# One head pair's loads in 14 DMAs instead of 30, key and value tiles laid out alike for both halves of a query tile, and a new order of issue

## The chip, the core and the metric

The kernel runs on one core of a Trainium2 chip. The metric is the device time of one execution in microseconds (us), the median of several runs; a profiled execution of the same program gives the trace. Engines are named as the profile names them: PE is the matrix engine (PEld its weight loads), DVE the vector engine, ACT the scalar engine, POOL GpSimd, SP the engine that here issues every DMA.

## The reference, cut to what matters

The inputs hold 4 batches of 8 heads. Each head has 512 local and 32 global queries, keys and values of 64 numbers, all float32.

```python
s_g   = scale * q_g @ [k_g, k_l].T                    # 32 global queries see all 544 keys
out_g = softmax(s_g) @ [v_g, v_l]
s_ll  = where(|i - j| <= 32, scale * q_l @ k_l.T, -1e9)  # 512 local queries: a band of 65 local keys ...
s_l   = [scale * q_l @ k_g.T, s_ll]                    # ... and the 32 global keys
out_l = softmax(s_l) @ [v_g, v_l]
x     = [out_g, out_l]                                 # 4 x 544 tokens of 512
h = x @ w_in;  x = (h * tanh(softplus(h))) @ w_out     # first feed-forward, 512 -> 2048 -> 512
h = x @ w2_in; out = (h * cos(h)) @ w2_out             # second feed-forward
```

The feed-forward weights arrive as 64-bit floats and are converted on the chip.

## The kernel before, in words

The work falls into two parts. **Attention** runs over 16 pairs of heads (`pp`, two heads of one batch; `NP` is 16). **Feed-forward** follows, in groups of two of the 16 blocks of the hidden width, each a product in three passes on rounded halves of the numbers (`l1` at L581 to L583, `l2` at L702). The first matmuls of the feed-forward (7 calls of `ff`) and the first 8 of 64 weight conversions (`c0` to `d5`, with loads at L137) are mixed into the attention part.

What a pair does, by the step names of the table `ORDER`: `lq` loads queries and keys (L292), `lv` loads values (L307). `Q` and `K` transpose them on PE, `q`, `k` and `h` copy the results out of PSUM. Queries lie in 4 tiles of 128 (`m`), each with two halves of 64 (`e`); a half sees 128 local keys and the 32 global ones, 160 columns. `S` (L370) makes the scores of two tiles of both heads in 8 matmuls, `X` masks and exponentiates, `ne`, `ni`, `N` and `NB` normalize (POOL and DVE), `TA` and `TB` transpose the probabilities of local and global keys, `ta` and `tb` copy them, and `AV` (L436) multiplies by the values: per half one matmul with local values (`ve` for even halves, `vo` for odd) and one with the global ones. For the global queries `SG`, `sm`, `st`, `se`, `ss`, `si`, `sn`, `TG` and `tg` do the same for two pairs at once (`m`), and `AG` multiplies by the values. `lg`, `G` and `g` load and transpose the global queries and keys of a batch, and `kg` copies the global keys into the key tile.

In the key tile `kw` the 160 columns of an even half are its 128 local keys and then the 32 global ones; an odd half's columns begin 64 further on, so that its global keys lie in the midst of its local ones. Its rows of probabilities have that order too, and therefore the value tiles have it: `vo` holds global values in its middle rows, and the 32 local values that come last lie in a fourth tile, `vx`. The keys are loaded shifted by 32, with wrap-around, in three pieces for each head.

What sets the order: each engine runs its instructions in the order in which the steps stand in `ORDER`, a table written into the code and read at L554. The letter behind a step's number puts its copy on ACT (`a`) or DVE (`d`). SP issues all DMAs in that order too, so a load that waits for its buffer holds up all loads behind it. Buffers: two for queries and keys (`qn`, `kn`, `kw`, `QT`), three for values. A value load therefore waits for `AV` and `AG` three pairs back.

Of the kernel before, what the change touches and what calls it, by code (L numbers as in the profile page):

```python
# [9 lines left out]
F32 = mybir.dt.float32  # L10
# [53 lines left out]
def kernel(  # L64
# [38 lines left out]
    def setup(mask):  # L103

        nc.gpsimd.memset(magic[:, 0:1], MAGIC)
        nc.gpsimd.memset(magic[:, 1:2], -MAGIC)
        nc.gpsimd.memset(mask, 0.0)
        band = [(0, 0, 128, 1, 0), (0, 0, 128, -1, 64), (64, 0, 64, 1, 0), (64, 96, 160, -1, 0)]
        for row, c0, c1, sgn, base in band:
            part = mask[row:row + 64, 1, c0:c1]  # L110
            nc.gpsimd.affine_select(
# [152 lines left out]
    def attention(ap, ps, pss, conv, tail):  # L264
# [12 lines left out]
        for t in kw:  # L277
            nc.vector.memset(t[:, NJ * W + 32:NJ * W + 64], 0.0)
# [552 lines left out]
```

## Time and profile before

| | |
|---|---|
| median of 3 runs | 1030.34 us (1029.53 to 1031.15) |
| profiled execution, its own time | 1031.32 us |
| its span, first to last instruction | 1028.4 us |
| PE busy | 918.7 us (89%) |
| DVE busy | 660.7 us (64%) |
| ACT busy | 455.9 us (44%) |
| POOL busy | 86.9 us (8%), all of it in the attention part |

The time of the profiled execution is 2.9 us longer than its span. Shares over the whole span say little here, since the attention part and the feed-forward part have different limits: the page's strip of slices shows PE at 3 to 7 tenths in the first quarter and at 9 after it. So each part is read by itself. "Waited for" in a row names the instruction that came last; idle time of an engine counts only where no other engine was the limit.

### The profile page before, as it was taken

Reading aid. Unit: us, or ns where it says so; the run is one execution under the profiler, and the core shown is the slowest. Engines: PE = TensorE matmul, PEld = TensorE weight load, DVE = VectorE, ACT = ScalarE, POOL = GpSimd, SP = SyncE. Lnnn points to the kernel's source line nnn. Section 1 sums busy time; section 2 is a strip of 40 time slices with the busy share of each in tenths; the row PEclk is TensorE's granted clock in tenths of the full one; section 3 lists DMA queues with packets and bytes.
Section 4 is the critical chain, followed back from the end, with each engine's and each line's share of the span. In section 5 each row is a group of like instructions: output and inputs, shape, how many; then the busy total and the mean of one; then the engine's idle time right before and its main releaser. Section 6 shows DMA issues by size and latency. Waiting matters only on the chain.

```text
span 1028.4 us, 16927 instructions
## 1 busy us (share of the span) xinstructions
PE 918.7 (89%) x6491; PEld 848.7 (83%) x6491; DVE 660.7 (64%) x1321; ACT 455.9 (44%) x907; POOL 86.9 (8%) x138
## 2 busy tenths in 40 slices
PE   4376665657889999999999999999999999999998
PEld 3254553546889999999999999999999999999997
DVE  2365634535599886878987784555655556666565
ACT  2154432524555444445443342554555554544443
POOL 3053422414000000000000000000000000000000
PEclk6668867868999999999999999999999999999999
DMA  3463343343233544597644457300000260000001
GB/s 81 97 146 85 71 96 78 70 97 71 74 103 98 169 164 162 191 345 290 199 148 158 147 164 265 124 1 1 1 1 1 98 230 1 32 31 32 1 31 51
DMA packets 117855, 108.06 MB, mean 105 GB/s; under 512 B 82832, under 2 KB 99216, under 8 KB 117776
## 3 DMA queue, kind: packets, MB, share of 16 engines
q1 hardware_dynamic: 117776, 107.00, 33.4%
q8 instruction: 51, 0.84, 0.3%
q14 instruction: 28, 0.23, 0.1%
HBM read 77.33 MB, written 29.62 MB: 104 GB/s over the span
## 4 chain that ended last, share of the span: by engine, by line
PE 78%; SPq 11%; DMA 4%; DVE 3%; issue 2%; ACT 1%; POOL 0%; POOLq 0%; ACTq 0%
PE acc L702 36%; PE h L581 12%; PE h L583 12%; PE h L582 12%; DMA qn<-in_q_l_dram 2%; SPq L323 2%; SPq L322 2%; SPq L318 1%; DMA cs<-in_moe_w_in_dram 1%; PE av L445 1%; PE av L449 1%; PE s L378 1%; SPq L317 1%; PE avg L517 1%; SPq L319 1%
## 5 line engine op out<-in xcount | busy, mean ns | idle before, releaser
L581 PE MATMUL h<-xl,w 128*128 128x384 f32 (+1 forms) x768 | 251.7, 328 | 2.9 <-DVE xl L571 2.9
L583 PE MATMUL h<-xh,w 128*128 128x384 f32 (+1 forms) x768 | 251.5, 327 | 0.0
L582 PE MATMUL h<-xh,w 128*128 128x384 f32 (+1 forms) x768 | 251.4, 327 | 0.0
L702 PE MATMUL acc<-gh,w 128*128 128x384 f32 (+1 forms) x768 | 186.0, 326 | 1.0 <-DVE w L219 1.0
L702 PE MATMUL acc<-w,gh 128*128 128x512 f32 x544 | 169.0, 392 | 0.0
L581 PEld LDWEIGHTS h<-xl,w 128*128 128x128 f32 x768 | 145.5, 189 | 5.1 <-DVE xl L571 3.2
L582 PEld LDWEIGHTS h<-xh,w 128*128 128x128 f32 x768 | 145.4, 189 | 1.8
L583 PEld LDWEIGHTS h<-xh,w 128*128 128x128 f32 x768 | 145.5, 189 | 0.0
L702 PEld LDWEIGHTS acc<-gh,w 128*128 128x128 f32 x768 | 135.5, 188 | 1.3 <-DVE w L219 1.3
L702 PE MATMUL acc<-gl,w 128*128 128x384 f32 (+1 forms) x384 | 125.1, 326 | 0.4 <-DVE xT L521 0.4
L702 PEld LDWEIGHTS acc<-w,gh 128*128 128x128 f32 x544 | 102.1, 188 | 20.5
L702 PE MATMUL acc<-w,gl 128*128 128x512 f32 x272 | 105.9, 389 | 0.0
L609 ACT ACTIVATE w<-h 128x768 f32<-128x768 f32 (+1 forms) x48 | 37.4, 778 | 142.3 <-PE h L583 137.1
L638 DVE SCALAR_TENSOR_TENSOR w<-w,h 128x768 f32<-128x768 f32 (+2 forms) x49 | 43.8, 894 | 71.4 <-ACT w L634 71.4
L628 DVE SCALAR_TENSOR_TENSOR w<-k,h 128x768 f32<-128x768 f32 (+2 forms) x49 | 43.8, 894 | 66.2 <-ACT k L627 66.2
L626 ACT ACTIVATE k<-h,magic 128x768 f32<-128x768 f32 (+2 forms) x49 | 41.9, 856 | 98.2 <-PE h L583 97.7
L345 PE MATMUL qt<-ident,qn 128*128 128x128 f32 x64 | 15.9, 399 | 74.8 <-DMA qn<-in_q_l_dram 74.8
L633 ACT ACTIVATE w<-w 128x768 f32<-128x768 f32 (+2 forms) x49 | 39.1, 798 | 89.1 <-DVE w L629 89.1
L345 PEld LDWEIGHTS qt<-ident,qn 128*128 128x128 f32 x64 | 11.0, 205 | 78.0 <-issue 61.8
L397 ACT ACTIVATE pr<-pr,nm 128x160 f32<-128x160 f32 x128 | 53.2, 418 | 48.4 <-DVE nm L394 46.3
L702 PEld LDWEIGHTS acc<-gl,w 128*128 128x128 f32 x384 | 72.4, 188 | 0.5 <-ACT xT L545 0.5
L614 DVE TENSOR_TENSOR gl<-w,gh 128x768 fp32r<-128x768 f32 (+1 forms) x48 | 43.6, 909 | 33.1 <-ACT gh L610 33.1
(115 smaller groups left out, 1405.7 us busy)
## 6 DMA issues: line engine op xcount, KB each, us to landing
scr<-co SPq DMA_DIRECT2D x48, 512.0 KB, 3.0
w<-scr SPq DMA_DIRECT2D x48, 512.0 KB, 5.3
cs<-in_moe_w_in_dram SPq DMA_DIRECT2D x32, 512.0 KB, 4.4
cs<-in_moe_w_out_dram SPq DMA_DIRECT2D x32, 512.0 KB, 4.2
out_dram<-o SPq DMA_DIRECT2D x17, 256.0 KB, 2.0
qn<-in_q_l_dram SPq DMA_DIRECT2D x32, 128.0 KB, 2.6
kn<-in_k_l_dram SPq DMA_DIRECT2D x32, 96.0 KB, 2.3
ve<-in_v_l_dram SPq DMA_DIRECT2D x32, 96.0 KB, 2.2
```

The costliest lines, as they stand in the source:

```text
L345: nc.tensor.transpose(t[:, j, :], qk[pp][0][:, j], ident)
L397: nc.scalar.activation(out=pr[:, i], in_=pr[:, i], func=AF.Exp, bias=nm[:, i:i + 1], scale=-1.0, accum_out=l[:, i:i + 1])
L581: nc.tensor.matmul(ps[:, c, 0:n], wh[:, k, :], xl[k], start=(k == 0), stop=False)
L582: nc.tensor.matmul(ps[:, c, 0:n], wh[:, k, :], xh[k], start=False, stop=False)
L583: nc.tensor.matmul(ps[:, c, 0:n], wl[:, k, :], xh[k], start=False, stop=(k == NK - 1))
L609: nc.scalar.activation(out=w, in_=h, func=AF.Mish)
L614: nc.vector.tensor_tensor(out=gl, in0=v["w"], in1=gh.bitcast(F32), op=ALU.subtract)
L626: nc.scalar.activation(out=k, in_=h, func=AF.Identity, scale=INV2PI, bias=magic[:, 0:1])
L628: nc.vector.scalar_tensor_tensor(out=t, in0=k, scalar=-C1, in1=h, op0=ALU.mult, op1=ALU.add)
L633: nc.scalar.activation(out=t, in_=t, func=AF.Sin, scale=0.5)
L638: nc.vector.scalar_tensor_tensor(out=t, in0=t, scalar=1.0, in1=h, op0=ALU.subtract, op1=ALU.mult, reverse0=True)
L702: nc.tensor.matmul(o, l, r, start=(g == 0 and m == 0), stop=(g == G - 1 and m == 5))
```

## The change

A pair is loaded in 14 DMAs. Keys come unshifted, one DMA for each head. Values of both heads are loaded together, in 6 DMAs for `ve` and `vo` and 4 for `vg`; the tile `vx` goes. The key tile becomes 8 blocks of 160 columns, one for each half, each with its local keys first and the global ones last; three copies fill the local part (`k`: blocks 1 to 3, the new step `k2`: blocks 4 to 6, `h`: 96 columns of blocks 0 and 7), and `kg` copies the global keys into 8 blocks instead of 4. With both halves ordered alike, `AV` does the global keys of a whole tile in one matmul of 128 columns for each head, ahead of the local ones. `SG` needs one more small matmul for each pair, since 32 local keys now come from the last block. `sn` moves from POOL to ACT or DVE, by its letter. The mask follows the new order. `ORDER` is a new table, 665 steps instead of 649; the number of conversions and of `ff` calls in it is the same.

```diff
 ORDER = """
-    hot:-1 hot:19 lq:0 setup lg:0 lv:0 Q:0 q:0a G:0 lq:1 g:0 K:0 k:0a kg:0 h:0a kg:1 S:0 lv:1 X:0 S:1 lq:2 Q:1 X:1 K:1
+    hot:-1 hot:19 lq:0 Q:0 K:0 q:0d lg:0 k:0a setup G:0 k2:0a g:0 c0:0 kg:0 lq:1 h:0a S:0 Q:1 c2:0 K:1 c1:0 kg:1 X:0
...
-        vx = [ap.tile([P, NJ - 1, 2, D], F32, name=f"vx{i}") for i in range(3)]
-        kw = [ap.tile([P, NJ * W + 64], F32, name=f"kw{i}") for i in range(2)]
+        kw = [ap.tile([P, 2 * NJ, W], F32, name=f"kw{i}") for i in range(2)]
...
             for h in range(2):
-                k = k_l[b, h0 + h]
-                nc.sync.dma_start(out=kn[32:P, 0, h], in_=k[0:P - 32])
-                nc.sync.dma_start(out=kn[:, 1:NJ, h, :], in_=k[P - 32:SL - 32].rearrange("(c p) d -> p c d", p=P))
-                nc.sync.dma_start(out=kn[0:32, 0, h], in_=k[SL - 32:SL])
+                nc.sync.dma_start(out=kn[:, :, h, :], in_=k_l[b, h0 + h].rearrange("(c p) d -> p c d", p=P))
...
         def load_v(pp):
...
+            v = v_l[b, 2 * p:2 * p + 2].rearrange("h s d -> (h s) d")
+            g = v_g[b, 2 * p:2 * p + 2]
+            both = v.rearrange("(c p) d -> p c d", p=P)
+            nc.sync.dma_start(out=E[32:P].rearrange("p h m d -> p (h m) d"), in_=both[0:P - 32])
             for h in range(2):
-                v, g = v_l[b, 2 * p + h], v_g[b, 2 * p + h]
-                rows = v.rearrange("(m p) d -> p m d", p=P)
-                nc.sync.dma_start(out=E[:, 1:NJ, h], in_=v[P - 32:SL - 32].rearrange("(m p) d -> p m d", p=P))
-                nc.sync.dma_start(out=E[32:P, 0, h], in_=v[0:P - 32])
-                nc.sync.dma_start(out=E[0:32, 0, h], in_=v[SL - 32:SL])
-                nc.sync.dma_start(out=O[0:64, :, h], in_=rows[32:96])
-                nc.sync.dma_start(out=O[96:P, :, h], in_=rows[96:P])
-                nc.sync.dma_start(out=O[64:96, :, h], in_=g[:, None, :].to_broadcast([SG, NJ, D]))
-                for jl in range(2):
-                    i = 2 * jl + h
-                    nc.sync.dma_start(out=G[32 * i:32 * i + 32, i], in_=g)
-                    nc.sync.dma_start(out=X[32 * i:32 * i + 32, jl:NJ - 1:2, h], in_=rows[0:32, jl + 1:NJ:2])
+                nc.sync.dma_start(out=E[0:32, h, 1:NJ], in_=both[P - 32:P, NJ * h:NJ * h + NJ - 1])
+            nc.sync.dma_start(out=E[0:SG, :, 0], in_=g.rearrange("h p d -> p h d"))
+            nc.sync.dma_start(out=O[0:P - 32].rearrange("p h m d -> p (h m) d"), in_=both[32:P])
+            nc.sync.dma_start(out=O[P - 32:P].rearrange("p h m d -> p (h m) d")[:, 0:2 * NJ - 1], in_=both[0:32, 1:2 * NJ])
+            for i in range(4):
+                nc.sync.dma_start(out=G[SG * i:SG * i + SG, i], in_=g[i % 2])
...
-        def k_copy(pp):
-            w, t = kw[pp % 2], live["k", pp]
-            copy("k", pp, w[:, 0:NJ * W].rearrange("p (m c) -> p m c", c=W)[:, :, 0:P], t)
-
-        def k_halo(pp):
-            w, t = kw[pp % 2], live["k", pp]
-            copy("h", pp, w[:, NJ * W:NJ * W + 32], t[:, 0, 0:32])
+        def k_copy(pp, j=1):
+            t = live["k", pp].rearrange("p a c -> p (a c)")
+            src = bass.AP(tensor=t.tensor, offset=t[:, 64 * j - 32:].offset, ap=[t.ap[0], [64, 3], [1, P]])
+            copy("k", pp, kw[pp % 2][:, j:j + 3, 0:P], src)
+
+        def k_copy2(pp):
+            k_copy(pp, 4)
...
         def av_pe(pp):
...
             for m in range(NJ):
                 jj, jl = divmod(m, 2)
+                for h in range(2):
+                    nc.tensor.matmul(av[pp][64 * h:64 * h + 64, m, :], G[:, 2 * jl + h, :], PB[pp][:, jj, :], start=True, stop=False)
                 for e in range(2):
                     cols = slice(64 * e, 64 * e + 64)
-                    last = e == 0 or m < NJ - 1
                     for h in range(2):
-                        nc.tensor.matmul(av[pp][64 * h:64 * h + 64, m, cols], (O if e else E)[:, m, h, :],
-                                         PA[2 * pp + jj][:, 2 * jl + h, cols], start=True, stop=not last)
-                    if last:
-                        for h in range(2):
-                            nc.tensor.matmul(av[pp][64 * h:64 * h + 64, m, cols], X[:, m, h, :] if e else G[:, 2 * jl + h, :],
-                                             PB[pp][:, jj, cols], start=False, stop=True)
+                        nc.tensor.matmul(av[pp][64 * h:64 * h + 64, m, cols], (O if e else E)[:, h, m, :],
+                                         PA[2 * pp + jj][:, 2 * jl + h, cols], start=False, stop=e == 1)
...
         def sg_norm(m):
-            nc.gpsimd.tensor_scalar(out=sgt, in0=sgt, scalar1=live["gr", m], scalar2=None, op0=ALU.mult)
+            if engine["at"] == "a":
+                nc.scalar.activation(out=sgt, in_=sgt, func=AF.Copy, scale=live["gr", m])
+            else:
+                nc.vector.tensor_scalar(out=sgt, in0=sgt, scalar1=live["gr", m], scalar2=None, op0=ALU.mult)
```

How this stands on the engines, at three places. First SP, in the first third of the attention part. Before, behind the query DMAs of one pair: the three key DMAs of its second head, then the first head's values (`ve`, `vo`, `vg`, `vx`), of which two more rows and the second head's ten follow.

```order
L302 DMA kn<-in_k_l_dram 96x64
L303 DMA kn<-in_k_l_dram 128x3x64
L304 DMA kn<-in_k_l_dram 32x64
L314 DMA ve_88<-in_v_l_dram 128x3x64
L315 DMA ve_88<-in_v_l_dram 96x64
L316 DMA ve_88<-in_v_l_dram 32x64
L317 DMA vo_91<-in_v_l_dram 64x4x64
L318 DMA vo_91<-in_v_l_dram 32x4x64
L319 DMA vo_91<-in_v_g_dram 32x4x64
L322 DMA vg_94<-in_v_g_dram 32x64
L323 DMA vx_97<-in_v_l_dram 32x2x64
```

Now SP at about the same place, queries and keys of a pair and then all values of a pair:

```order
L301 DMA qn<-in_q_l_dram 128x4x64 x2
L303 DMA kn<-in_k_l_dram 128x4x64 x2
L315 DMA ve_88<-in_v_l_dram 96x8x64
L317 DMA ve_88<-in_v_l_dram 32x3x64 x2
L318 DMA ve_88<-in_v_g_dram 32x2x64
L319 DMA vo_91<-in_v_l_dram 96x8x64
L320 DMA vo_91<-in_v_l_dram 32x7x64
L322 DMA vg_94<-in_v_g_dram 32x64 x4
```

Fourteen issues stand where 30 stood; the largest, of 96x8x64, are twice the size of any value DMA before. Over the whole program SP's list has 293 rows in place of 596.

Second PE, at the `AV` step of the third pair. Before, behind the `AG` step of another pair, the matmuls of one query tile (`ve` and `vo` local values, `vg` and `vx` global ones and the rest; `PA`, `PB` the transposed probabilities):

```order
L517 MATMUL avg<-PG,ve_89 64x32 x8
L517 MATMUL avg<-PG,vo_92 64x32 x2
L445 MATMUL av<-PA,ve_90 64x64 x2
L449 MATMUL av<-PB,vg_96 64x64 x2
L445 MATMUL av<-PA,vo_93 64x64 x2
L449 MATMUL av<-PB,vx_99 64x64 x2
```

Now, the same work of one query tile of another pair, behind a transpose and a score step:

```order
L425 MATMUL ta<-ident,pr 128x128 x4
L382 MATMUL s<-kw_98,QT 64x160 x8
L446 MATMUL av<-PB,vg_94 64x128 x2
L450 MATMUL av<-PA,ve_88 64x64 x2
L450 MATMUL av<-PA,vo_91 64x64 x2
```

Two matmuls of 128 columns stand in place of four of 64; the last tile of a pair had no `vx` rows before, so a pair goes from 30 matmuls to 24.

Third ACT. Before, a key copy and its 32 columns (`kw<-kt`), a query copy and the exponentials of the global queries (`sg`), then those of the local ones (`pr`); the multiplication of `sg` by `gr` (L494) stood on POOL:

```order
L545 COPY kw_100<-kt 128x4x128
L545 COPY kw_100<-kt 128x32
L545 COPY QT<-qt 128x512
L482 ACTIVATE sg,gl<-sg_1124,gnm 128x512
L483 ACTIVATE sg,gl<-sg_1125,gnm 128x32
L397 ACTIVATE pr,l<-pr,nm 128x160 x8
```

Now, a stretch of ACT's list with the same kinds of work:

```order
L142 ACTIVATE ca<-cs 128x512
L550 COPY QT<-qt 128x512
L550 COPY kw_98<-kt 128x3x128
L497 ACTIVATE sg<-sg,gr 128x640
L401 ACTIVATE pr,l<-pr,nm 128x160 x4
L550 COPY PB<-tb 128x256
```

A key copy of 384 columns (one of two, with a third of 192) and the multiplication of `sg` stand on ACT; over the part, six of the eight multiplications are on ACT and two on DVE.

## Rows read from the trace of the kernel before

**Rows 1.** The view by windows: attention up to the first second-layer matmul of the feed-forward, the 28.6 us behind it, and the rest. Columns: window, length, busy time of each engine (instructions), granted PE clock, share of the DMA engines, GB/s.

```profile
0.00:271.40 271.40, 169.72 (x2273) 134.32 (x2274) 127.33 (x490) 104.52 (x367) 86.89 (x138) 0.77 0.38 89
271.40:300.00 28.60, 25.71 (x139) 25.39 (x138) 23.84 (x42) 14.66 (x29) 0.00 (x0) 0.94 0.24 74
300.00:1028.40 728.40, 723.28 (x4083) 688.98 (x4081) 509.52 (x790) 336.72 (x513) 0.00 (x0) 1.00 0.33 112
```

**Rows 2.** The view of waits in the attention part: engine and line, what it waited for, us in total, times, longest.

```profile
PE qt L345 <- DMA qn<-in_q_l_dram: 74.8, 11, 10.1
...
PE av L449 <- DMA vg<-in_v_g_dram: 5.3, 3, 2.5
...
PE av L445 <- DMA ve<-in_v_l_dram: 2.1, 1, 2.1
```

**Rows 3.** SP's timeline: start, length, issue. A conversion load, then one pair from its query DMAs on, and the next pair's; last the first conversion load behind all attention loads, with the wait for its buffer.

```profile
34.35 1.73 SPq L137 DMA_DIRECT2D cs<-in_moe_w_in_dram  x1
...
175.43 0.97 SPq L299 DMA_DIRECT2D qn<-in_q_l_dram  x2
176.50 0.45 SPq L302 DMA_DIRECT2D kn<-in_k_l_dram  x1
176.99 0.43 SPq L303 DMA_DIRECT2D kn<-in_k_l_dram  x1
177.46 0.48 SPq L304 DMA_DIRECT2D kn<-in_k_l_dram  x1
...
181.00 0.61 SPq L317 DMA_DIRECT2D vo<-in_v_l_dram  x1
181.65 0.60 SPq L318 DMA_DIRECT2D vo<-in_v_l_dram  x1
182.29 0.43 SPq L319 DMA_DIRECT2D vo<-in_v_g_dram  x1
...
190.10 0.97 SPq L299 DMA_DIRECT2D qn<-in_q_l_dram  x2
...
261.20 22.73 SPq L137 DMA_DIRECT2D cs<-in_moe_w_in_dram  x4
```

**Rows 4.** SP's own waits over the whole run: the longest in total of those that belong to loads of a pair (waited for, us in total, times, longest).

```profile
SPq L314 <- PE avg L517: 3.5, 1, 3.5
```

**Rows 5.** PE's timeline: the first `S` step of the run, the first and last instructions of one `AV` step, the two kinds of matmul of an `SG` step, and a `Q` and an `S` step behind a wait. Columns: start, length, form, count, and in brackets the idle time before with what ended it.

```profile
9.21 1.83 PE L378 MATMUL s<-kw,QT 64*64 64x160 f32 x18 [0.75 <-ACT kw L545]
...
84.24 0.34 PE L445 MATMUL av<-PA,ve 128*64 128x64 f32 x4
...
85.92 0.29 PE L445 MATMUL av<-PA,vo 128*64 128x64 f32 x4
...
88.94 0.31 PE L463 MATMUL sg<-kw,qz 128*64 128x32 f32 x4
89.08 1.06 PE L466 MATMUL sg<-kw,qz 128*64 128x512 f32 x4
...
100.55 1.09 PE L345 MATMUL qt<-ident,qn 128*128 128x128 f32 x4 [9.39 <-DMA qn<-in_q_l_dram]
101.57 1.35 PE L378 MATMUL s<-kw,QT 64*64 64x160 f32 x16
```

**Rows 6.** The view by windows again, columns as in Rows 1: two stretches in which loads were ahead, a third at full clock, and a starved one.

```profile
51.40:90.60 39.20, 32.99 (x464) 25.11 (x464) 30.10 (x118) 24.57 (x93) 20.43 (x29) 0.80 0.47 113
...
72.00:91.00 19.00, 18.61 (x303) 15.01 (x301) 16.10 (x67) 12.06 (x47) 10.53 (x16) 0.86 0.24 54
183.00:200.00 17.00, 14.35 (x228) 10.34 (x227) 11.73 (x53) 10.33 (x41) 8.61 (x14) 0.99 0.32 72
...
140.00:160.00 20.00, 10.50 (x138) 7.99 (x138) 7.72 (x35) 5.71 (x25) 5.47 (x10) 0.73 0.39 93
```

**Rows 7.** Groups of instructions of the attention part, by line and form: busy us and mean ns, then idle time before and what ended it. Two of PE, then copies on DVE and ACT, exponentials on ACT, and three of POOL.

```profile
L360 PE MATMUL kt<-ident,kn 128*128 128x128 f32 x64 | 11.6, 310 | 3.7 <-DMA kn<-in_k_l_dram 1.3 <-issue 1.2 <-DVE nm L394 0.6
...
L333 PE MATMUL gt<-ident,gq 64*128 64x64 f32 x16 | 2.0, 254 | 1.3 <-DMA gq<-in_k_g_dram 1.2
...
L547 DVE COPY kw<-kt 128x512 f32<-128x512 f32 x7 | 4.8, 684 | 2.6 <-PE kt L360 2.6
...
L547 DVE COPY PB<-tb 128x256 f32<-128x256 f32 x8 | 3.3, 415 | 1.2 <-PE tb L430 1.1
...
L547 DVE COPY kw<-kt 128x32 f32<-128x32 f32 x11 | 2.0, 181 | 0.5 <-ACT kw L545 0.5
...
L397 ACT ACTIVATE pr<-pr,nm 128x160 f32<-128x160 f32 x128 | 53.2, 418 | 48.4 <-DVE nm L394 46.3 <-POOL pb L415 1.8 <-POOL pr L410 0.2
...
L545 ACT COPY kw<-kt 128x512 f32<-128x512 f32 x9 | 5.3, 584 | 7.7 <-PE kt L360 7.6
...
L410 POOL TENSOR_TENSOR pr<-pr,r 128x512 f32<-128x512 f32 x32 | 35.3, 1103 | 31.8 <-DVE r L406 28.1 <-DVE kw L547 1.8 <-PE ta L421 1.3
L494 POOL TENSOR_SCALAR sg<-sg,gr 128x640 f32<-128x640 f32 x8 | 16.2, 2028 | 12.8 <-DVE gr L491 12.7
...
L355 POOL COPY kw<-kG 128x128 f32<-128x128 f32 x15 | 4.7, 328 | 24.6 <-PE sg L463 15.9 <-PE s L378 3.4 <-DVE kG L340 3.2
```

**Rows 8.** DMA issues of the page: KB each, and median us from issue to landing.

```profile
qn<-in_q_l_dram SPq DMA_DIRECT2D x32, 128.0 KB, 2.6
...
ve<-in_v_l_dram SPq DMA_DIRECT2D x32, 96.0 KB, 2.2
```

More of the change, by code (lines that the diff above doesn't have):

```diff
@@ L107, in setup @@
         nc.gpsimd.memset(mask, 0.0)
[L108 to L111, printed above, removed]
-                out=part, in_=part, pattern=[[sgn, c1 - c0]], compare_op=ALU.is_ge, fill=NEG,
-                base=base, channel_multiplier=-sgn)
+        for row in (0, 64):
+            for sgn, base in ((1, 0), (-1, 64)):
+                part = mask[row:row + 64, 1, 0:P]
+                nc.gpsimd.affine_select(
+                    out=part, in_=part, pattern=[[sgn, P]], compare_op=ALU.is_ge, fill=NEG,
+                    base=base, channel_multiplier=-sgn)
         for m in (0, 2):
@@ L116, in setup @@
         nc.gpsimd.memset(mask[0:64, 0, 0:32], NEG)
[L117 removed]
+        nc.gpsimd.memset(mask[64:128, 2, 96:128], NEG)
     slots = {}
@@ L277, in attention @@
         for t in kw:
-            nc.vector.memset(t[:, NJ * W + 32:NJ * W + 64], 0.0)
+            nc.vector.memset(t[:, 0, 0:32], 0.0)
+            nc.vector.memset(t[:, 2 * NJ - 1, 96:128], 0.0)
         nc.vector.memset(sgt[:, SL:SL + P], 0.0)
-        for t in vg + vx:
+        for t in vg:
             nc.gpsimd.memset(t, 0.0)
+        for t in vo:
+            nc.gpsimd.memset(t[96:P, 1, NJ - 1], 0.0)
         NP = B * NPAIR
@@ L459, in sg_pe @@
             t0 = pss[0].tile([P, NJ, P], F32, tag="s", name="sg0", bufs=3)
-            t1 = ps_t([P, SG], "sg1")
+            t1 = ps_t([P, 2 * SG], "sg1")
             live["sg", m] = t0, t1
             for c in range(2):
-                nc.tensor.matmul(t1[64 * c:64 * c + 64], qz[b % 2][:, p + c, :], kw[c][:, P:W], start=True, stop=True)
+                for i, at in enumerate((P, 64)):
+                    nc.tensor.matmul(t1[64 * c:64 * c + 64, SG * i:SG * i + SG], qz[b % 2][:, p + c, :], kw[c][:, 2 * NJ - 1, at:at + SG], start=True, stop=True)
             for c in range(2):
-                keys = kw[c][:, 0:NJ * W].rearrange("p (m c) -> p m c", c=W)[:, :, 0:P]
-                nc.tensor.matmul(t0[64 * c:64 * c + 64], qz[b % 2][:, p + c, :], keys, start=True, stop=True)
+                nc.tensor.matmul(t0[64 * c:64 * c + 64], qz[b % 2][:, p + c, :], kw[c][:, 0:2 * NJ:2, 0:P], start=True, stop=True)
         def sg_max(m):
```

91 lines of the change are left out of this document (48 added, 43 removed).

## The prediction

> **What bounds the kernel now.** I read the run by parts, then the waits of the busiest engine, then the queue that it waits for.
>
> The windows part the run [rows 1]. From 271.4 us on, PE is busy 25.71 + 723.28 = 749 of 757 us: PE is the limit there, and the change touches nothing in it. In the first 271.4 us PE is busy 169.72 us at a mean granted clock of 0.77, DVE 127.33, ACT 104.52, POOL 86.89, and the DMA engines 38%. No engine is near full, so something between them is the limit.
>
> PE is idle 271.4 - 169.7 = 101.7 us there. The waits say for what [rows 2]: 74.8 us at `Q` for the query DMA, in 11 waits of up to 10.1 us, and 5.3 + 2.1 us at `AV` for values. Two groups add 1.3 us for keys and 1.2 us for global ones [rows 7]. Loads together cost PE 84.7 us; all else leaves 17.0 us.
>
> Why do queries come late? In SP's timeline one issue follows another about 0.47 us apart, with hardly a gap [rows 3], and SP's own waits for a free buffer are 3.5 us at the line that waits longest [rows 4]. The pair that begins at 175.43 holds SP until 190.10. Thirty issues of 0.42 to 0.61 us make 14.1 us, and 16 pairs 226 of the 261.2 us after which SP is through [rows 3]. A query DMA lands 2.6 us after its issue [rows 8], so the landing is short; what is late is the issue, behind twenty value DMAs. **SP's issuing bounds the attention part**, at 271.4 / 16 = 17 us for each pair.
>
> **The change, part by part.** *SP.* A pair has 14 issues. The four of queries and keys have shapes the trace shows, 0.49 us apart: 2.0 us. Of the ten for values the four `vg` are known, and 32-row pieces cost 0.43 to 0.60 us. A 96x8x64 issue isn't in the trace. Nearest are the three-dimensional value issues of 0.60 and 0.61 us, and above them the longest conversion issue without a wait, 1.73 us [rows 3]. I take 0.61, since 128x4x64 (0.49) isn't dearer than 32x4x64 (0.60): cost doesn't follow size. Ten value issues come to 4.8 us, a pair to 6.8 us, 16 pairs to 109 us. With 8 global loads (3.7 us), 8 conversion loads (some 6 us) and half of the odd stalls before (261 - 226 - 10 = 25 us, so 13 us), SP needs about 132 us instead of 261. The work that was behind it now counts.
>
> *PE.* Its work in the part is 169.72 us at 0.77, or 131 us at full clock. `AV` goes from 30 matmuls of 64 columns to 16 of 64 and 8 of 128. At full clock 15 groups of two take 85.92 - 84.24 = 1.68 us plus the last, 0.12 us each [rows 5]; a doubled column count makes 16 such units, so +0.12 us a pair, +2 us in all: no saving, since columns cost and not matmuls. From below, an instruction's fixed share could save: 6 of 30 matmuls, at most 0.35 us a pair. `SG` gets as many small matmuls again, 0.14 us a step [rows 5], +1 us. Sum 134 us at full clock (126 to 134).
>
> *DVE.* Before it made 7 key copies at 684 ns and 11 of 32 columns at 181, 6.8 us; now 15 of 384 columns and 10 of 192. Between the 256-column row (415) and the 512-column row [rows 7] I estimate 550 and 350 ns: 11.8 us, +5.0. At the rates of these rows, three `QT`, three `PB`, one `xT` copy and one conversion step that go to ACT or behind the part take off 2.1 + 1.2 + 0.7 + 0.8 = 4.8. Two `sn` come at some 0.8 us: +1.6. Net +2, so 129 us.
>
> *ACT.* 17 key copies at an estimated 480 ns and 6 at 280 make 9.8 us against 6.2: +3.6. Copies taken over +1.7, one conversion step less -0.6, six `sn` at about 0.7 us +4.2. Sum 104.5 + 9 = 113 us.
>
> *POOL.* The eight `sn` of 2.03 us go (-16.2 us); fifteen `kg` copies double from 328 ns (+4 to 5 us) [rows 7]. Sum 75 us. `sn` also leaves a chain: POOL waited 12.7 us for it.
>
> *The rest of the run.* Conversions and `ff` calls in the table are the same, so I price the 757 us at 0, covered by PE being busy in 749 of them; one or two us either way.
>
> **How long the part becomes.** PE and DVE are now the largest, and both have a record of what they reach when loads are ahead [rows 6]. By PE: in 72 to 91 us it was busy 98% at a clock of 0.86. 134 / 0.86 = 156 us, plus the 17 us of waits that weren't loads, is 173. By DVE: 30.10 of 39.2 us busy from 51.4 to 90.6, 77%, so 129 / 0.77 = 168. I take **170 us**, a gain of 101 us.
>
> The bounds: at a clock of 0.99, as from 183 to 200 [rows 6], PE needs 135 us, and with some 10 us of start, since the first scores begin at 9.21 [rows 5], the part can't end ahead of 145. At 0.73, as from 140 to 160, PE needs 184 us, with the 17 us 201.
>
> The profiled execution took 1031.3 us, 1.0 above the median, so I count from the median: 1030.3 - 101 = **929 us**; bounds 1030.3 - 126 = 904 and 1030.3 - 70 = 960.
>
> **The rivals.**
>
> *PE stays at its lower clock.* The new order leaves short gaps, and PE runs much of the part at 1.2 GHz, as in the starved stretch. For it: even in 51.4 to 90.6 the clock was 0.80. Against: where PE had no waits of 8 us for queries, the clock was 0.86 to 0.99 [rows 6]. At the part's own 0.77: 134 / 0.77 + 17 = 191, a gain of 80: 950 us, up to the 960 above.
>
> *The large issues are dear.* Two 96x8x64 issues a pair at 1.73 us instead of 0.61 add 16 x 2 x 1.12 = 36 us to SP's 132, 168 us, and then 10 us of tail as before (271.4 - 261.2): 178, but with the starved pattern left in parts, some 185: 944 us. Against it stands that no row's issue time grows with size.
>
> *The transfers were the limit, not the issues.* The bytes hardly change, so the part would stay 271 us: about 1030 us, no change. Against it: the DMA engines are busy 38% of the part [rows 1]; in 170 us the same bytes would make it some 60%. The Trainium skill, in "DMA: Bandwidth & Descriptors", section "Issuing engines are not separate DMA queues", speaks for this rival: the time on the sequencer to start a DMA "is usually small relative to the DMA itself". The trace doesn't bear that out here, since one issue after another at 0.47 us apart outlasts landings of 2.2 to 2.6 us that overlap.
>
> *SP blocks itself: slower than before.* A value load waits for `AV` and `AG` three pairs back, and the next pair's query DMA is queued behind it on SP, with PE, DVE and ACT waiting for that. If each pair became one chain: 6.8 us of issue, 2.6 of landing, `Q` 1.1 and `S` 1.35 [rows 5], four exponentials 1.7, one `pr` of POOL 1.1 [rows 7], three copies at 0.6, `TA` some 1, `AV` 1.8: 19 us. It decides from 17 us a pair on; at 19 us the part is 304 us and the time 1063 us. Against it: in the new table every value load stands at least 21 steps behind the steps it waits for, at 170 / 665 = 0.26 us a step some 5 us.
>
> That the change doesn't do what it says is excluded by SP's list: 293 rows against 596.
>
> **How the numbers follow.** Forecast (part of 145 to 185 us, 904 to 944) 0.74; lower clock 0.16; dear issues 0.06; transfers 0.02; self-blocking 0.02. The range of 904 to 960 takes in the first three as priced and leaves out the last two and what lies beyond the bounds, less than 2 in 10. A measurement of this kernel can tell about 0.2% (2 us) from no change. Faster 0.74 + 0.16 + 0.06 = 0.96, same 0.02, slower 0.02.
>
> **What would show it.** SP's timeline: 14 issues a pair, about 7 us, with waits for `AV` or `Q` now between them; the 96x8x64 issue at 0.4 to 0.7 us. PE's wait for query DMAs down from 74.8 to under 15 us. The first second-layer matmul at about 170 us instead of 270.4. In that part PE busy over 80% at a clock above 0.8, DVE busy about 129 us, POOL 75. From there to the end 757 us as before. The forecast is wrong if `Q` still waits for loads while SP issues without gaps, if the part ends after 200 us with PE's clock at 0.77 or lower, or if the feed-forward part changes its length by more than a few us.

## The result, and the profile after

| | before | changed |
|---|---|---|
| median, us (lowest to highest, runs) | 1030.74 (1029.53 to 1033.55, 4) | 923.34 (922.06 to 924.07, 4) |
| profiled execution, us (its span) | 1031.3 (1028.4) | 924.07 (922.3) |
| first matmul of the second layer, us | 270.4 | 164.9 |
| from there to the end of the span, us | 758.0 | 757.4 |

The ratio is 0.8953 (95% interval 0.8932 to 0.8975): 107 us less, or 10.5%. Nearly all of it lies in the attention part, which ends 105.5 us sooner; the rest keeps its length to 0.6 us.

Windows of the changed kernel, cut where the second layer begins. The columns are length, then busy time and count of PE, PEld, DVE, ACT and POOL, PE's mean granted clock, the DMA engines' share and GB/s; they answer to [rows 1].

```profile
0.00:164.94 164.94, 137.79 (x2108) 112.78 (x2109) 129.14 (x495) 111.34 (x385) 74.42 (x130) 0.94 0.65 141
193.50:922.30 728.80, 724.07 (x4087) 689.80 (x4085) 509.96 (x791) 336.78 (x513) 0.00 (x0) 1.00 0.33 112
```

PE now is busy 137.79 of 164.94 us, 84%, at a clock of 0.94 instead of 0.77. Its idle time fell from 101.7 us to 27.2. In units of full clock its work is 137.79 x 0.94 = 129.5 us, before 131. This product is rough: for kernels below with the same matmuls it comes to between 125 (e1) and 133 us (e11). So far as it can tell, the work is the same, and both the waits and the clock gave time back. Behind the part, in the second row, PE is busy 724.07 of 728.80 us as before. The DMA share rose from 0.38 to 0.65, with nearly the same bytes in less time.

PE's waits in that part (line, what it waited for, total us, times, longest), which answer to [rows 2]:

```profile
PE qt L344 <- DMA qn<-in_q_l_dram: 7.7, 3, 6.5
PE kt L358 <- DMA kn<-in_k_l_dram: 6.8, 4, 4.4
PE av L446 <- DMA vg<-in_v_g_dram: 5.8, 2, 4.3
PE s L382 <- DVE kw L353: 1.4, 1, 1.4
PE tg L504 <- ACT sg L497: 1.2, 1, 1.2
```

Waits for loads are 20.3 us instead of 84.7, and spread over queries, keys and global values. They are few and long (up to 6.5 us). All other waits come to some 7 us. So the loads are still what PE waits for most.

SP's timeline of one pair, from its queries on (start, duration, line, operation, what is loaded, how many issues), which answers to [rows 3], and the first issue behind the last pair:

```profile
83.61 1.83 SPq L322 DMA_DIRECT2D vg<-in_v_g_dram  x4
85.49 0.97 SPq L301 DMA_DIRECT2D qn<-in_q_l_dram  x2
86.51 1.86 SPq L303 DMA_DIRECT2D kn<-in_k_l_dram  x2
88.42 0.50 SPq L315 DMA_DIRECT2D ve<-in_v_l_dram  x1
88.96 1.01 SPq L317 DMA_DIRECT2D ve<-in_v_l_dram  x2
90.02 0.43 SPq L318 DMA_DIRECT2D ve<-in_v_g_dram  x1
90.49 0.42 SPq L319 DMA_DIRECT2D vo<-in_v_l_dram  x1
90.96 0.54 SPq L320 DMA_DIRECT2D vo<-in_v_l_dram  x1
91.54 3.48 SPq L322 DMA_DIRECT2D vg<-in_v_g_dram  x4
...
152.25 0.39 SPq L138 DMA_DIRECT2D cs<-in_moe_w_in_dram  x1
```

Three things are to be seen. The large issue, 96x8x64 at L315 and L319, takes 0.42 to 0.50 us, no more than one of 32 rows. Two `kn` take 1.86 us here where two `qn` take 0.97, and four `vg` 3.48 where they took 1.83 a pair ahead: odd stalls of 0.9 and 1.7 us in this pair. And one issue still follows another with hardly a gap; SP is through with its pairs at 152 us, not at 132.

Groups of the changed kernel in that part (busy us, mean ns), which answer to [rows 7]; the last two lines are the page's rows of DMA issues (KB, us to landing), which answer to [rows 8]:

```profile
L552 DVE COPY kw<-kt 128x384 f32<-128x384 f32 x15 | 8.2, 549 | 12.0 <-PE kt L358 11.7
L550 ACT COPY kw<-kt 128x384 f32<-128x384 f32 x17 | 7.7, 477 | 6.6 <-PE kt L358 5.2 <-DVE kw L552 1.3
L353 POOL COPY kw<-kG 128x256 f32<-128x256 f32 x15 | 7.4, 495 | 13.3 <-DVE nm L398 5.8 <-PE s L382 4.7 <-DVE kG L339 2.4
L497 ACT ACTIVATE sg<-sg,gr 128x640 f32<-128x640 f32 x6 | 5.0, 830 | 0.0
L552 DVE COPY kw<-kt 128x192 f32<-128x192 f32 x10 | 3.5, 346 | 1.1 <-ACT kw L550 1.1
```

```profile
qn<-in_q_l_dram SPq DMA_DIRECT2D x32, 128.0 KB, 2.9
ve<-in_v_l_dram SPq DMA_DIRECT2D x16, 192.0 KB, 4.1
```

### The profile page after: what moved, and what is told of

Its sections match the earlier page's. It is cut to its first block, busy times and chain, and to the rows that moved or that the text cites. A ratio compares the mean times of both kernels' runs of the same rounds, so it can differ in the third digit from the quotient of the medians.

```text
span 922.3 us, 16347 instructions
## 1 busy us (share of the span) xinstructions
PE 887.5 (96%) x6331; PEld 827.9 (90%) x6331; DVE 662.2 (72%) x1326; ACT 464.2 (50%) x928; POOL 74.4 (8%) x130
## 4 chain that ended last, share of the span: by engine, by line
PE 88%; DVE 3%; DMA 3%; SPq 3%; ACT 1%; issue 1%; POOL 0%; ACTq 0%; DVEq 0%; POOLq 0%
PE acc L707 40%; PE h L586 13%; PE h L588 13%; PE h L587 13%; DMA kn<-in_k_l_dram 2%; PE av L446 1%; PE av L450 1%; PE s L382 1%; PE ta L425 1%; SPq L322 1%; DMA vg<-in_v_g_dram 1%; DMA ve<-in_v_l_dram 1%; PE kt L358 1%; ACT pr L401 1%; SPq L301 1%
## 5 line engine op out<-in xcount | busy, mean ns | idle before, releaser
L157 DVE SCALAR_TENSOR_TENSOR ct<-ca,ct 128x512 f32<-128x512 f32 x64 | 44.3, 691 | 28.2 <-ACT ca L142 27.4
L707 PEld LDWEIGHTS acc<-w,gl 128*128 128x128 f32 x272 | 51.1, 188 | 9.6
```

The costliest lines, as they stand in the source:

```text
L157: nc.vector.scalar_tensor_tensor(out=t.bitcast(F32), in0=a.bitcast(F32), scalar=TINY * TINY, in1=t.bitcast(F32), op0=ALU.is_ge, op1=ALU.mult)
L707: nc.tensor.matmul(o, l, r, start=(g == 0 and m == 0), stop=(g == G - 1 and m == 5))
```

## The experiments

**Theory.** SP's issuing bounded the part before and, more weakly, still bounds it after: an issue costs SP some 0.45 us whatever its size, and the fourteen issues that each pair lost are the gain. **Rivals.** (a) The bytes, or the shape of the pieces, cost the time and not the issues. (b) The new order and the one `SG` matmul for both halves made the gain, not the DMAs. (c) After the change PE, DVE and ACT hold the part by their chain, and SP no longer counts.

"Part" is the time from the span's start to the first matmul of the second layer; the rest of the span was 756 to 758 us in every one of these kernels. e1 to e4 were run once each, e5 and e6 twice.

A pair of the kernel before has 28 issues, not the 30 that the title, the prediction and two of the expectations give: 2 for queries, 6 for keys and 20 for values. Its trace has 448 in 16 pairs, and 633 in the whole run against 409 in the changed kernel. So the change saves 14 a pair, 224 in all.

| kernel | issues of a pair on SP | part, us | PE idle in it, us | PE clock | DMA share | time, us |
|---|---|---|---|---|---|---|
| before | 28 | 270.4 | 101.7 (to 271.4) | 0.77 | 0.38 | 1030.7 |
| e3 new order on before | 28 | 268.1 | 109.6 | 0.76 | 0.39 | 1027.6 |
| e1 change, loads cut up as before | 28 | 257.3 | 96.3 | 0.77 | 0.39 | 1015.9 |
| e4 change, `vg` in eight | 18 | 191.7 | 45.3 | 0.88 | 0.58 | 951.1 |
| e2 change, old order | 14 | 171.0 | 25.1 | 0.91 | 0.61 | 929.1 |
| changed | 14 | 164.9 | 27.2 | 0.94 | 0.65 | 923.3 |
| e11 two `vg` on POOL | 12 | 155.2 | 17.6 | 0.97 | 0.71 | 914.1 |
| e6 `vg` of pairs 3 to 15 left out | 10 | 148.1 | 12.6 | 0.97 | 0.73 | 907.2 |
| e5 all values of these left out | 4 | 146.0 | 12.1 | 0.98 | 0.48 | 905.3 |

**e1: the loads cut back, all else changed.** `kn` three pieces a head, the large `ve` and `vo` four each, the 32-row `vo` four, global `ve` two:

```diff
-                nc.sync.dma_start(out=kn[:, :, h, :], in_=k_l[b, h0 + h].rearrange("(c p) d -> p c d", p=P))
+                for c0, c1 in ((0, 1), (1, 3), (3, NJ)):
+                    nc.sync.dma_start(out=kn[:, c0:c1, h, :], in_=k_l[b, h0 + h].rearrange("(c p) d -> p c d", p=P)[:, c0:c1])
-            nc.sync.dma_start(out=E[32:P].rearrange("p h m d -> p (h m) d"), in_=both[0:P - 32])
+            for c in range(0, 2 * NJ, 2):
+                nc.sync.dma_start(out=E[32:P].rearrange("p h m d -> p (h m) d")[:, c:c + 2], in_=both[0:P - 32, c:c + 2])
```

> The changed kernel with each pair's loads cut into 30 DMAs again, the same bytes into the same tiles, all else as changed. If the number of issues is what the change saved (theory), SP again needs about 14 us a pair, 226 us with 40 us of other loads and odd stalls, the attention part ends near 270 us, and the run takes 1010 to 1035 us. If the new order, the tile layout or the shorter PE and POOL work made the gain (rival), it stays under 960. If the transfer of the bytes were the limit, it stays at 923.

Measured: 1015.93 us, a part of 257.3. The same bytes to the same places, in 28 issues instead of 14, take 92.4 us of the gain of 105.5 back: 0.41 us for each of the 224 issues. The 13.1 us that are left are what the order, the layout, `AV` and `sn` together gain while SP is full. Rival (a) falls as far as bytes go. SP's timeline of e1 shows the issues in an all but unbroken chain, about one every half microsecond:

```profile
131.99 1.90 SPq L323 DMA_DIRECT2D vo<-in_v_l_dram  x4
133.94 1.88 SPq L325 DMA_DIRECT2D vo<-in_v_l_dram  x4
135.85 1.81 SPq L327 DMA_DIRECT2D vg<-in_v_g_dram  x4
137.71 1.05 SPq L301 DMA_DIRECT2D qn<-in_q_l_dram  x2
138.81 2.95 SPq L304 DMA_DIRECT2D kn<-in_k_l_dram  x6
```

Each of the four `vo` at L323 carries a quarter of what the one issue at L319 (0.42 us) carries in the changed kernel. The Trainium skill ("DMA: Bandwidth & Descriptors", section "Issuing engines are not separate DMA queues") says that the time to start a DMA is usually small beside the DMA itself. If it were so here, e1 would take the changed kernel's 923 us. It took 1015.93, so it isn't so for pieces like these.

**e2 and e3: the order and the loads apart.** e2 is the changed code with the old order (`k2` right behind its `k`, `sn` lettered as in the change); e3 is the code before with the new order, and a `k2` that does nothing:

```diff
 e2
-ORDER = """ (the new table)
+ORDER = """ (the old table, with k2:n behind each k:n)
 e3, in the code before
-ORDER = """ (the old table)
+ORDER = """ (the new table)
+            "k2": lambda _: None,
```

> The changed kernel with the order table of before (the second key copy put right behind the first, and the letters of the new table for the multiplication of the global probabilities). Theory (issues saved, order secondary): 925 to 955 us, since SP still has 14 issues a pair. Rival (the new order made the gain): over 980.

> The kernel before with the new order table and nothing else of the change (the second key copy does nothing there). Theory: SP still issues 30 DMAs a pair, 1020 to 1045 us. Rival (order): 980 or less.

Measured: e2 929.09 us with a part of 171.0, e3 1027.64 with 268.1. On the old loads the order alone shortens the part by 2.3 us, which one run can't tell from noise (runs of the kernel before lay between 1026.95 and 1033.92 us); on the new ones it is worth 6.1. Rival (b) falls. What the order does is seen in PE's waits of e2, where only 6.3 us are for loads but 18.5 for all else, as on DVE and ACT ahead of `S`:

```profile
PE qt L344 <- DMA qn<-in_q_l_dram: 5.6, 3, 2.0
PE s L382 <- DVE nm L398: 4.0, 3, 2.1
PE avg L522 <- ACT sg L485: 2.1, 1, 2.1
PE s L382 <- DVE kw L552: 2.0, 3, 1.2
```

With the new order most of these are gone, and PE runs into the loads sooner.

**e4: four issues more.**

```diff
-                nc.sync.dma_start(out=G[SG * i:SG * i + SG, i], in_=g[i % 2])
+                for r in range(0, SG, 16):
+                    nc.sync.dma_start(out=G[SG * i + r:SG * i + r + 16, i], in_=g[i % 2][r:r + 16])
```

> The changed kernel with the four loads of global values cut into eight of 16 rows, so 18 issues a pair instead of 14, same bytes. If SP's issuing still sets the attention part after the change, 64 more issues at 0.47 us are 30 us of SP, and the run is 20 to 30 us longer, 943 to 953. If PE and DVE set it now, SP has slack and the run is at most 7 us longer, 923 to 930.

Measured: 951.08 us, a part of 191.7. Sixty-four issues more, of half the size, cost 26.8 us, 0.42 each, which is what one takes on SP (0.42 us is also the median of the 128 issues of 16 rows in its trace). All of it reaches the end: rival (c) falls. PE's waits for loads go from 20 to 34 us and its clock from 0.94 to 0.88.

**e5 and e6: what the part takes when SP has less to issue.** In both, the values of the first three pairs stay in their buffers and are used again by pairs 3 to 15, so what is computed isn't the reference.

```diff
 e5, in load_v
+            if pp >= 3:
+                return
 e6, in load_v
-            for i in range(4):
+            for i in range(4 if pp < 3 else 0):
```

> The changed kernel without the value loads of pairs 3 to 15: the values of the first three pairs stay in their buffers and are used again, so the output is not the reference's. It asks what the attention part would take if SP's queue were out of the way. SP loses 13 x 10 issues, some 4.8 us a pair and the odd stalls with them, 62 us or more of its 152. Theory (issuing on SP still holds up the part): PE's 129.5 us of full-clock work at a clock of 0.94 to 0.99, with the 7 us of waits that aren't loads, give a part of 138 to 147 us instead of 165, so 896 to 906 us, and no wait of PE for loads above 2 us in sum. Rival (the chain through DVE, ACT and PE holds the part, and the load waits would come back as other waits): 918 to 924 us.

> The changed kernel without the four loads of global values into vg for pairs 3 to 15 (52 issues fewer; the values of the first three pairs are used again, so the output is not the reference's). At the 0.43 us an issue that the eight-piece version showed, SP loses 22 us, with its odd stalls perhaps 35. Theory (SP's issuing holds up the part by about 20 us): 900 to 908 us, nearly all that can be had. Rival (what SP gives is only part of it): 912 to 920 us.

Measured: 905.26 and 907.24 us. The window of e5 up to the second layer, and below it that of e6, with the columns as above:

```profile
0.00:146.00 146.00, 133.94 (x2108) 108.39 (x2109) 128.79 (x495) 111.03 (x385) 74.83 (x130) 0.98 0.48 111
```

```profile
0.00:148.10 148.10, 135.51 (x2107) 110.64 (x2108) 128.24 (x495) 111.07 (x385) 74.56 (x130) 0.97 0.73 155
```

With loads out of the way the part takes 146 us: PE is busy 92% of it at 0.98. That is close to PE's own limit, and PE's waits for loads are down to 2.2 us. So the value loads of these pairs cost the changed kernel some 19 us, bytes and issues together. e6 tells issues from bytes once more: it moves nearly all the bytes, at 155 GB/s instead of 141, and takes only 2 us more than e5. It leaves out 52 small issues (0.4 of the 107 MB of the whole run) and gains 16.8 us, so nearly all of the 19 us is issues. That is 0.32 each, less than one takes, likely because PE is then near its own limit.

**e7, e8, e11 and e12: the same issues on another queue.** The `vg` loads on POOL or on ACT, all four of a pair (e7, e8) or two (e11, e12):

```diff
-                nc.sync.dma_start(out=G[SG * i:SG * i + SG, i], in_=g[i % 2])
+                nc.gpsimd.dma_start(out=G[SG * i:SG * i + SG, i], in_=g[i % 2])                       # e7; e8 has nc.scalar
+                (nc.sync if i < 2 else nc.gpsimd).dma_start(out=G[SG * i:SG * i + SG, i], in_=g[i % 2])  # e11; e12 has nc.scalar
```

> The changed kernel with the four vg loads of a pair issued by POOL instead of SP; all else the same. SP loses 64 issues, 28 us at 0.43 us each; POOL, busy 74 of 165 us, has 90 us free. Theory: the waits of PE for loads fall from 20 us to under 5 and the time comes to 903 to 912 us, faster than both kernels. Rival (a DMA that POOL issues costs POOL more than SP, or POOL's steps then come late for the masked products that PE and DVE wait for): 920 us or more, with waits for POOL in place of the waits for loads.

> The changed kernel with the four vg loads of a pair issued by ACT instead of SP. SP loses 28 us as when POOL issues them, but ACT, busy 111 us of the part, gets some 64 x 0.43 = 28 us more and comes to 139. Theory (relief on SP counts): 905 to 915 us. Rival (ACT's exponentials, for which POOL and PE wait, come late): 918 us or more.

> The changed kernel with two of a pair's four vg loads on POOL and two left on SP. With all four on POOL, PE's load waits fell from 20 to 8 us but other waits rose from 7 to 17, with POOL's busy time up by 32 us (0.5 us an issue). With half, POOL gets 16 us and SP loses 32 issues, 14 us. Theory (both queues have room then): load waits of 8 to 12 us, other waits of 8 to 11, a part of 155 to 160 us, 912 to 918 us. Rival (issues on POOL delay what PE waits for as much as they spare on SP, however many): 919 to 923 us.

> The changed kernel with two of a pair's four vg loads on ACT's queue and two left on SP. With all four on ACT, load waits fell from 20 to 10 us, other waits rose from 7 to 12, and PE's clock stayed at 0.94. Theory (half the load on ACT disturbs it half as much): a part of 156 to 161 us, 914 to 919 us. Rival (what SP spares ACT gives back): 920 to 924 us.

| | time, us (lowest to highest, runs) | ratio to before (interval) | part, us |
|---|---|---|---|
| e7 four on POOL | 920.92 (918.71 to 921.46, 4) | 0.8927 (0.8898 to 0.8955) | 161.5 |
| e8 four on ACT | 922.39 (920.37 to 924.11, 4) | 0.8947 (0.8921 to 0.8973) | 162.6 |
| e11 two on POOL | 914.08 (911.95 to 915.96, 5) | 0.8867 (0.8843 to 0.8891) | 155.2 |
| e12 two on ACT | 923.63 (919.65 to 924.65, 5) | 0.8950 (0.8927 to 0.8973) | 162.9 |

For e7, e8 and e12 my theory was wrong: their intervals overlap that of the changed kernel (0.8932 to 0.8975). e11 is faster than both kernels, 9 us below the changed one, with intervals that don't meet.

Why not e7? On POOL an issue is busy time, as POOL's timeline shows in a stretch of e7:

```profile
83.18 0.86 POOL L353 COPY kw<-kG 128x256 f32<-128x256 f32 x1
84.14 0.32 POOL L489 TENSOR_SCALAR gl<-gl 128x1 f32<-128x1 f32 x1
84.52 2.03 POOL L322 DMA_DIRECT2D vg<-in_v_g_dram  x4
86.56 0.63 POOL L419 TENSOR_TENSOR pb<-pr,r 128x256 f32<-128x256 f32 x1
```

Four take 2.03 us, and POOL's busy time rises by 32 us. SP has slack then, waiting for the `AV` three pairs back, and PE waits for POOL and for `vg` that POOL issued late. SP's waits, then two of PE's, in e7:

```profile
SPq L315 <- PE avg L522: 14.3, 4, 7.8
SPq L315 <- PE av L450: 14.2, 3, 6.4
```

```profile
PE av L446 <- DMA vg<-in_v_g_dram: 5.6, 1, 5.6
PE ta L425 <- POOL pr L414: 4.5, 4, 2.5
```

With two on each (e11) SP lost 32 issues and POOL gained 16 us; PE's waits for loads fell to 5.9 us, all its waits to 17.5:

```profile
0.00:155.20 155.20, 137.63 (x2108) 112.86 (x2109) 131.90 (x495) 110.36 (x385) 90.40 (x162) 0.97 0.71 150
```

Why not ACT? ACT's issues in a stretch of e8, and SP's of the same time:

```profile
88.27 0.36 ACTq L322 DMA_DIRECT2D vg<-in_v_g_dram  x1
...
88.73 0.38 ACTq L322 DMA_DIRECT2D vg<-in_v_g_dram  x1
...
89.15 0.91 ACTq L322 DMA_DIRECT2D vg<-in_v_g_dram  x2
```

```profile
87.35 1.22 SPq L317 DMA_DIRECT2D ve<-in_v_l_dram  x2
90.13 0.31 SPq L318 DMA_DIRECT2D ve<-in_v_g_dram  x1
90.48 0.43 SPq L319 DMA_DIRECT2D vo<-in_v_l_dram  x1
92.30 0.31 SPq L320 DMA_DIRECT2D vo<-in_v_l_dram  x1
```

While ACT issues four, from 88.27 to 90.06, SP issues nothing between 88.57 and 90.13, and nothing again from 90.91 to 92.30. It waits for landings. In the trace's records the landing of each load of SP and of ACT is told by one of eight semaphores (counters that engines wait on), taken in turn by both, and a load doesn't start before the load that last used its semaphore has landed. The `ve` at 90.13 has the semaphore of ACT's `vg` of 88.27, which landed at 90.11; the `vo` at 92.30 has that of the second `vg` of the row of 89.15, which landed at 92.28. Two of SP's waits in e8:

```profile
SPq L320 <- DMA ve<-in_v_l_dram: 6.1, 4, 2.7
SPq L318 <- DMA vg<-in_v_g_dram: 2.4, 2, 1.5
```

SP's waits for landings in the part come to 34.9 us in e8 and 23.3 in e12, against 3.3 in the changed kernel. Issues on POOL have eight semaphores of their own, and there SP waits 0.5 us (e7) and 5.3 us (e11). So what SP is spared by ACT's issues it loses in waits for landings; whether ACT would help with semaphores of its own, no run tells. ACT's busy time stays at 110.8 us instead of the 139 expected, since an issue on its queue isn't counted as busy.

The Trainium skill, in "Perfetto Trace Analysis", section "DMA Instruction — HWDGE (DVE, Sync)", tells of a block that generates descriptors, is shared by two sequencers (DVE's and SP's) and is locked while one uses it, and it counts the wait for the lock in a row's time. No such wait between ACT and SP shows in these runs: in e12, two of ACT's issues (0.32 us at 87.58 and 0.38 us at 88.00) fall beside a row of two of SP's at 87.18, and that row takes 1.01 us, as it does in the changed kernel.

**e9 and e10: two small terms.** `sn` back on POOL, and the global keys' matmuls of `AV` in halves, 32 of 64 columns instead of 16 of 64 and 8 of 128:

```diff
 e9
-            if engine["at"] == "a":
-                nc.scalar.activation(out=sgt, in_=sgt, func=AF.Copy, scale=live["gr", m])
-            else:
-                nc.vector.tensor_scalar(out=sgt, in0=sgt, scalar1=live["gr", m], scalar2=None, op0=ALU.mult)
+            nc.gpsimd.tensor_scalar(out=sgt, in0=sgt, scalar1=live["gr", m], scalar2=None, op0=ALU.mult)
 e10, per half e, cols = slice(64 * e, 64 * e + 64)
+                        nc.tensor.matmul(av[pp][64 * h:64 * h + 64, m, cols], G[:, 2 * jl + h, :],
+                                         PB[pp][:, jj, cols], start=False, stop=True)
```

> The changed kernel with its eight sn back on POOL (2.03 us each), instead of six on ACT (0.83 us) and two on DVE (0.66 us). POOL comes from 74 to 90 us busy of 165, ACT from 111 to 106. Theory (SP's issuing holds the part, POOL has room; moving sn is worth little): 922 to 929 us, at most some 5 us slower. Rival (sn on POOL was a part of the gain, since PE waited for sg behind pr): over 930 us.

> The changed kernel with the global keys' matmuls of AV cut back into halves: 32 matmuls of 64 columns an AV instead of 16 of 64 and 8 of 128, the same columns in all. Theory (a matmul's time goes with its columns, as the prediction priced it): 921 to 926 us, within 2 us of the changed kernel. Rival (an instruction has a fixed share, 0.06 us each, the bound that the prediction gave): 16 x 8 x 0.06 = 7 us more where PE holds the part, 926 to 931 us.

Measured: e9 927.59 us (924.35 to 929.0, 5 runs; ratio 0.8987, 0.8963 to 0.9010), with a part of 168.3; e10 922.43 (921.85 to 923.79, 4 runs; 0.8947, 0.8926 to 0.8969), with a part of 164.1. In e9 PE waits 2.5 us for `sg` and 5.3 for `pr` on POOL, so the move off POOL is likely worth 3 to 4 us; its interval still touches that of the changed kernel. e10 shows no difference in time: it has 128 matmuls more (two records of the profile each), PE's busy time is 1.6 us longer, and its waits for loads 3.2 us shorter, 17.1 us. As loads still hold the part up, a cost of that size could be hidden. The two groups, first of the changed kernel and then of e10:

```profile
L446 PE MATMUL av<-PB,vg 128*64 128x128 f32 x256 | 28.7, 295 | 6.1 <-DMA vg<-in_v_g_dram 5.8 <-ACT xT L550 0.2
```

```profile
L451 PE MATMUL av<-PB,vg 128*64 128x64 f32 x512 | 33.5, 231 | 1.6 <-DMA vg<-in_v_g_dram 1.6
```

The matmuls overlap one another, so their modelled durations (295 against 231 ns for half the columns) aren't a price.

## Why the prediction was right, point by point

**The bound was named rightly.** SP's issuing held the part, and the number of issues decides: e1 gives back 92 of 105 us with the issues alone, e3 shows 2.3 us without them (one run, within the noise), and e4 prices one more at 0.42 us. The thirty issues of the prediction are 28, but its 14.1 us a pair hold: issues begin some 0.51 us apart, and the pair that it shows takes 14.7 us.

**929 against 923.3: several sizes were off and partly cancel, so that the closeness is in part luck.**

- *SP, 132 us foreseen, 152 measured.* The issues themselves came out: 14 a pair at about 6.75 us against 6.8, and the unknown 96x8x64 at 0.31 to 0.54 us against the 0.61 taken (30 of the 32; the other two, at 1.84 and 1.56, hold a stall). But I halved the odd stalls along with the issues, to 13 us. Out of 152 us, 16 x 6.75 = 108 are pairs, some 10 are other loads, and some 11 are waits for buffers and completions; 23 us remain as stalls, about as many as before (25). They don't scale with the number of issues. The trace shows what they go with: the view of the DMA queues has 17 packets of 16 KB of the kind `instruction` in the part (18 before), and 16 of the 25 issues over 0.7 us overlap one (17 of 21 before, 17 of 19 in e1). In the pair shown above such packets run from 86.47 to 87.40, under the `kn`, and from 92.79 to 94.18, under the `vg`. Of the other nine, five lie in the first 16 us. That the packets are the cause wasn't tested by a run.
- *So loads still counted.* I had put PE's load waits under 15 us and none in the sum; they are 20.3 us. "With waits for `AV` or `Q` now between them" came true only here and there: SP's waits for `AV` and `AG` are 4.8 us, and else it issues with hardly a gap. That half of my own sign of failure was met, queries waiting while SP issues without a pause, but for 7.7 us instead of 74.8. e5 prices what the value loads still cost at 19 us.
- *PE's clock, 0.86 foreseen, 0.94 measured.* 129.5 / 0.86 would have been 151 us of busy time; it was 138. I took the clock from a stretch of the starved kernel. Over the kernels of the table the clock falls, by and large, as PE's idle time rises: 0.98 at 12 us idle, 0.88 at 45, 0.77 at 96. It isn't set by that sum alone: at 25 to 27 us idle it lies between 0.91 (e2) and 0.97 (e7).
- *Other waits, 17 us foreseen, 7 measured.* e2, with the old order, still has 18.5. With the new order they are gone: I carried over a number that belonged to the order that the change replaces.
- *PE's work, 134 foreseen, 129.5 by busy time and clock.* As that product is off by some 4 us either way (125 in e1, 133 in e11), the +2 us for `AV` and +1 for `SG` can be neither seen nor excluded. For `AV`, e10 fits that columns and not matmuls cost, to within the 1.6 us above.
- In sum: 156 + 17 = 173, taken as 170, against 137.8 + 7 + 20.3 = 165. The clock and the other waits were too dear by 28 us, the loads too cheap by 20. That these two nearly cancel is luck.

**The other engines.** DVE's 129.14 us met the 129 foreseen, at 78% of the part against the 77% of the second route to the forecast; ACT's 111.3 the 113, POOL's 74.4 the 75; the key copies took 549 and 346 ns against estimates of 550 and 350. Rows of the same operation at nearby sizes were enough for these.

**The rivals.** *Lower clock*: didn't come, since the loads come sooner. It was the right thing to fear: with four issues a pair more (e4) the clock is at 0.88, with fourteen (e1) at 0.77. *Dear large issues*: excluded by 0.31 to 0.54 us; the conversion issue of 1.73 us from which I priced this rival overlaps such a packet in the trace of the kernel before (34.57 to 35.71), and so was likely a stall. *Transfers*: excluded by e1 and e6. *SP blocking itself*: its longest waits for `AV` were 2.2 us; it takes a queue with slack, as in e7, to see waits of 7.8 us.

## What to carry to other kernels

Count the DMA issues of a queue and multiply by the measured time of one: where the product is near the stage's length, the number of issues bounds the stage, and fewer and larger DMAs buy their number times that time until the next engine is the limit. Ask what that limit is by leaving the loads out, before spending work on more. When a queue is full, a second helps only if its engine has time to spare and its loads don't make the first wait: look at what their landings are told by. Here two issues a pair on POOL, with semaphores of its own, gained 9 us, four gave most of that back, and none gained on ACT, which shares eight with SP.

## What of the hardware was not expected

- An issue takes SP about the same time whether it carries 16 rows of a `vg` (e4: median 0.42 us of 128) or 96x8x64 (0.31 to 0.54 us for 30 of 32).
- Issues on ACT's queue make SP wait for landings, as the loads of both share eight semaphores (34.9 us in e8, 23.3 in e12). Issues on POOL, with eight others, hardly do (0.5 us in e7, 5.3 in e11), at 0.5 us of POOL's busy time each.
- Odd stalls of SP's issues of about a microsecond go with packets of 16 KB of the kind `instruction`: 16 of 25 in the changed kernel, 17 of 19 in e1.
- Idle time of PE costs more than itself: from the changed kernel to e4 PE's idle time rises by 18 us and its busy time by 8.6, at a clock of 0.88 instead of 0.94.
- With POOL busier by its issues, DVE's busy time rose from 129.1 to 131.9 (e11) and 134.8 us (e7), while copies out of PSUM kept their 674 ns. It shows in conversion steps, as in this group of the changed kernel and below it of e7 (both from 0 to 155 us). In e7 the two longest of that group, 2458 ns at 38.79 and 3140 ns at 105.08, lie beside POOL's multiplications at L414 and L419; beside POOL's issues alone such steps take 714 and 1139 ns, and beside nothing on POOL 678 to 694. So it seems to be POOL's element-wise work, moved in time, more than the issues themselves; no run parts the two.

```profile
L152 DVE SCALAR_TENSOR_TENSOR ct<-cs,ct 128x512 int32<-128x512 int32 x8 | 6.6, 820 | 0.0
```

```profile
L152 DVE SCALAR_TENSOR_TENSOR ct<-cs,ct 128x512 int32<-128x512 int32 x8 | 10.4, 1296 | 0.0
```
